# Gelu's tanh form: three ScalarE and three VectorE operations replaced by one activation and one product

## The chip, the cores and the metric

The kernel runs on one core of one Trainium2 chip. That core has five engines that matter here: TensorE (PE, with weight loads listed as PEld), VectorE (DVE), ScalarE (ACT), GpSimd (POOL) and SyncE (SP), which issues the transfers. The metric is device time of one execution in microseconds; the kernel before takes 2557.23 us, the median of three runs (2554.48 to 2558.53). Profiles come from one execution each.

## The reference

`x` is 2048 rows of 576 numbers. It is normalised (`xn`), and two branches read `xn`: an attention with 32 heads of 18 numbers, and a gated feed-forward with 4608 hidden numbers. The result joins them:

```python
def _gelu(x):
    return jax.nn.gelu(x, approximate=True)
def _B_ref(x, w_gate, w_up, w_down):
    return (_gelu(x @ w_gate) * (x @ w_up)) @ w_down
xn = _layernorm(x, axis=-1)
s = _A_ref(xn, A_wqkv, A_wo)
g = _silu(_B_ref(xn, B_w_gate, B_w_up, B_w_down))
return x + s * g
```

With `approximate=True`, gelu(g) is 0.5 g (1 + tanh(0.79788 (g + 0.044715 g^3))). The silu is y sigmoid(y), which equals 0.5 y (1 + tanh(y / 2)).

## The kernel before

**Stages.** A prologue normalises and transposes `x` and projects q, k and v (to DRAM). Then come 144 feed-forward *sections*: 4 blocks of 512 rows, times 18 parts of 256 hidden numbers, times 2 halves (`g` 0 and 1) of 128. The first 11 sections run alone or with a few attention maxima; the next 128 each carry a quarter of one of 32 attention units (4 heads by 512 queries); the last 5 are in the epilogue, with the output projection.

**One section with attention.** PE runs 27 pairs of matmuls into `pgu`, one PSUM tile of two banks: `pg` (gate sums) and `pu` (up sums). Among them `spread` places 8 score pairs (`pe`, line 897) and 8 pairs for row maxima (`pm`, line 851). ACT takes each `pe` with an Exp of 128x1024 into `pT` (line 898); DVE takes each `pm` with a maximum reduction (line 852). At the end PE multiplies the 16 probability tiles with the values into `acc` (line 914). In the first quarter of a unit `acc` is put away by a ScalarE Copy (line 918), in the other three it is added to `accs` on DVE (line 920).

**Down projection.** After every second section, the halves of a part being complete, PE runs seven products `py` (line 525), which DVE adds to the seven sums `M` (line 575); in the first part of a block ScalarE or DVE copies them (lines 573, 571). `sums_a` and `cut_a` form the operands of these products from `h` on POOL (lines 456 to 461 and 447, 448). While the first block (and some parts of the second) runs, the section that also holds the down products forms its down weights: three ScalarE Copies into `T` (lines 495, 497, 498), the last of which has to wait until the products have read the old `T`. The 32 maxima of a unit are closed by lines 858, 861, 862 and a DVE transpose (867), one hand to the other, on DVE, POOL and DVE.

**PSUM.** `pgu`, `pe`, `pm`, `acc` and `py` share one ring of four tiles (`ring`, `RING = 4`). `pgu` holds a tile through its section and until `activate` has read it for the last time.

**The place of the change.** `activate` turns `pgu` into `h` at the end of each section: Square of `pg` (ACT, line 428); (square + 1/GC) times `pg` (DVE, 429); a Copy of `pu` out of PSUM (ACT, 432), times `pg` (DVE, 433), which frees the ring tile; Tanh with scale GC GS (ACT, 434); (tanh + 1) times that product (DVE, 436). The result is twice gelu(gate) times up. So `M` holds twice the sums of the reference, and silu's Tanh has scale 0.25, its product the factor 0.25. `last_section` in the epilogue does the same with three DVE operations behind the Square and the Tanh (lines 1130 to 1134).

**What sets the order.** PE's and SP's orders are those of the program text. ACT, DVE and POOL are ordered by a planner from its own costs in attention (`keep_in_program_order` fixes some places), by the program text in the epilogue.

Of the kernel before, what the change touches and what calls it, by code (L numbers as in the profile page):

```python
# [8 lines left out]
F32 = mybir.dt.float32  # L9
F32R = mybir.dt.float32r  # L10
AF = mybir.ActivationFunctionType
ALU = mybir.AluOpType
# [5 lines left out]
P = 128  # L18
NT = S // P
TB = 512  # L20
# [36 lines left out]
ADD, SUB = ALU.add, ALU.subtract  # L57
COMBINED = (((6, ADD, 0), (5, ADD, 0)), ((6, SUB, 3), (5, ADD, 2)), ((6, SUB, 4), (5, SUB, 1)), ((4, ADD, 2), (1, SUB, 3)))
EPS = 1e-5
GC = 0.044715  # L60
GS = 0.7978845608028654
SCALE = DH ** -0.5


# [24 lines left out]
def kernel(ctx: ExitStack, tc: tile.TileContext, x, wqkv, wo, w_gate, w_up, w_down, out):  # L89
# [331 lines left out]

        return [lambda i=i: pair(i) for i in range(len(terms))], pg, pu

    def activate(pg, pu, g, early):

        h = ffn.tile([P, 3 + 3 * g, TH], F32, name=f"h{g}", bufs=2 - g)
        t1 = h[:, 0:2].rearrange("p a t -> p (a t)")
        nc.scalar.activation(t1, pg, AF.Square)
        nc.vector.scalar_tensor_tensor(t1, t1, 1.0 / GC, pg, op0=ALU.add, op1=ALU.mult)  # L429
        if early:  # L430
            t2 = ffn.tile([P, TB], F32, name="t2", bufs=1)
            nc.scalar.activation(t2, pu, AF.Copy)  # L432
            nc.vector.tensor_tensor(t2, t2, pg, op=ALU.mult)  # L433
        nc.scalar.activation(t1, t1, AF.Tanh, scale=GC * GS)
        if early:
            FF["last"] = lambda: nc.vector.scalar_tensor_tensor(t1, t1, 1.0, t2, op0=ALU.add, op1=ALU.mult)
        else:
            nc.vector.scalar_tensor_tensor(t1, t1, 1.0, pg, op0=ALU.add, op1=ALU.mult)
            nc.vector.tensor_tensor(t1, t1, pu, op=ALU.mult)
        return h  # L440


# [173 lines left out]
    def section(specials=(), slots=False):  # L616

        n = FF["n"]
        FF["n"] += 1
        b, r = divmod(n // G, NR)  # L620
        g = n % G
        keep = tc.keep_in_program_order
        pairs, pg, pu = gate_up()
        hooks, FF["hooks"] = FF["hooks"], {}

        def hook(i, what):
            hooks.setdefault(i, []).append(what)

        for i in range(n + 1, min(n + 3, NF)):
            if i not in FF["raw"]:  # L630
                FF["raw"][i] = load_gu(gu_part(i))
        nxt = FF["raw"].pop(n + 1, None)
        one = split_ap if n + 1 < ATT.start else split
        if nxt:
            for k in range(NG - 1):
                split_gu(nxt, k, one)
        if n == 0:
            load_rawd(0)
        if g == 0 and (b, r) in FORMED:
            raw = FF["rawd"]  # L640
            hook(12, lambda: sums_b(raw))
        new = n + 1 < NF and (n + 1) % (NR * G) == 0
        xd = []
        if new:
            for k in range(NG - 1):
                hook(9 * k + 9, lambda k=k: xd.append(load_xd(b + 1, k)))
        for p in spread(pairs, specials, 1 if slots else None, hooks):
            p()
        if nxt:
            split_gu(nxt, NG - 1, one)  # L650
        if n == 0:
            cut_plain_b(FF["rawd"])
        FF["w"] = nxt
        FF["act"] = activate(pg, pu, g, n < ATT.stop)
        if g > 0 or n not in ATT:
            FF.pop("last", lambda: None)()
        if new:
            xd.append(load_xd(b + 1, NG - 1))
            for t in hooks.get(len(pairs), ()):
                t()  # L660
            FF["xd"] = xd
# [5 lines left out]
    def finish():  # L667

        n = FF["n"] - 1
        b, r = divmod(n // G, NR)  # L670
        g, h, s = n % G, FF["act"], part(b, r)
        pool, vec, act = nc.gpsimd, nc.vector, nc.scalar
        keep = tc.keep_in_program_order
        FF.pop("last", lambda: None)()

        def hook(i, what):
            FF["hooks"].setdefault(i, []).append(what)

        def behind(what):
            what(keep if (n + 1) % (NR * G) == 0 else lambda i: i)  # L680

        late = (n + 2) % (NR * G) == 0 and n + 2 < NF
        if g == 1 and (b, r + 1) in NEXT:
            load_rawd(part(b, r + 1))
        if b == 0 and r < PLAIN:
            if g == 0 and r > 0:
                raw = FF["rawd"]
                hook(4, lambda: cut_plain_b(raw))
            cut_plain(g, h)
        elif (b, r) in FORMED:  # L690
            lead = n < ATT.start
            if g == 0:
                if lead:
                    hook(6, lambda: high_b(0))
                    hook(12, lambda: high_b(1))
                else:
                    high_b(0)
                    high_b(1)
                hook(9 if lead else 2, lambda: low_b(0))
                hook(16 if lead else 10, lambda: low_b(1))  # L700
                for k, i in enumerate((19, 24) if lead else (1, 3) if late else (13, 20)):
                    hook(i, lambda k=k: t_piece(s, k, True))
                sums_a(g, h, vec if lead else pool)
                hook(12, lambda: cut_a(0, h, pool, pool, keep))
            else:
                for k, i in enumerate((2, 9)):
                    hook(i, lambda k=k: t_piece(s, 2 + k, True))
                behind(lambda k: (sums_a(g, h, pool, k), cut_a(1, h, pool, pool, keep)))
        else:
            if g == 0:  # L710
                for k, i in enumerate((None, 5, 27, 27) if late else (None, 5, 13, 21)):
                    if i is None:
                        t_piece(s, k)
                    else:
                        hook(i, lambda k=k: t_piece(s, k))
            behind(lambda k: (sums_a(g, h, pool, k), cut_a(g, h, pool, pool, k)))
        if g == G - 1:
            FF["down"].append((b, r, n + 1))
# [54 lines left out]
    def gate(k, i):  # L773

        y, t = (t[:, i] for t in SC)
        nc.scalar.activation(t, y, AF.Tanh, scale=0.25)
        nc.gpsimd.tensor_tensor(t, t, y, op=ALU.mult)
        nc.gpsimd.tensor_tensor(y, y, t, op=ADD)

# [227 lines left out]
    with tc.tile_pool(name="epi", bufs=1, reuse_waits="tile") as epi:  # L1007
# [45 lines left out]
        def gate(k):  # L1053
            if gated <= k < len(groups) and groups[k][0] < NB - 1:
                yy = YY[k % len(YY)]
                th = ffn.tile([P, D], F32, name="th", tag="h0", bufs=2)
                act.activation(th, yy, AF.Tanh, scale=0.25)
                vec.scalar_tensor_tensor(yy, th, 1.0, yy, op0=ADD, op1=ALU.mult)

        def project(k):  # L1060
# [11 lines left out]
        def multiply(k, po, c):  # L1072
            b, j = groups[k]
            t = YY[k % len(YY)].rearrange("p (c d) -> p c d", c=2)
            if b < NB - 1:
                vec.scalar_tensor_tensor(t[:, c], t[:, c], 0.25, po[:, c, 0:DC], op0=ALU.mult, op1=ALU.mult)
            else:
                for i in range(2)[c]:
                    m = QUARTERS[2 * (j // 2) + i][2]
                    vec.scalar_tensor_tensor(t[:, i], FF["M"][:, m, j % 2], 0.25, po[:, i, 0:DC], op0=ALU.mult, op1=ALU.mult)  # L1080

        def finish_rows(k, c):
            t, xx = (a[k % len(a)][:, DC * c.start:DC * c.stop] for a in (YY, XX))
# [26 lines left out]
        def last_section():  # L1110

            n = FF["n"]
            FF["n"] += 1
            g = n % G
            pairs, pg, pu = gate_up()
            hooks, FF["hooks"] = FF["hooks"], {}
            nxt = FF["raw"].pop(n + 1, None)
            if nxt:
                split_gu(nxt, 0)
                split_gu(nxt, 1)  # L1120
            for t in spread(pairs, (), 1, hooks):
                t()
            if nxt:
                split_gu(nxt, 2)
            FF["w"] = nxt
            h = ffn.tile([P, 3 + 3 * g, TH], F32, name=f"h{g}", bufs=2 - g)
            t1 = h[:, 0:2].rearrange("p a t -> p (a t)")

            def gelu():
                act.activation(t1, pg, AF.Square)  # L1130
                vec.scalar_tensor_tensor(t1, t1, 1.0 / GC, pg, op0=ADD, op1=ALU.mult)
                act.activation(t1, t1, AF.Tanh, scale=GC * GS)
                vec.scalar_tensor_tensor(t1, t1, 1.0, pg, op0=ADD, op1=ALU.mult)
                vec.tensor_tensor(t1, t1, pu, op=ALU.mult)

            return h, gelu
# [83 lines left out]
        gate(n)  # L1220
        for i, c, m in QUARTERS:
            t = ffn.tile([P, 2, DC], F32, name="tg", tag=("h0", "h1")[c], bufs=2 - c)
            act.activation(t, M[:, m], AF.Tanh, scale=0.25)
            vec.scalar_tensor_tensor(M[:, m], t, 1.0, M[:, m], op0=ADD, op1=ALU.mult)
            for k in range({6: 1, 4: 2}.get(m, 0)):
                step()
# [30 lines left out]
```

## Time and profile before

| | |
|---|---|
| median of three runs | 2557.23 us |
| the profiled execution | 2556.38 us, its span 2554.6 us |
| granted TensorE clock | 0.998 |
| PE busy / PEld busy | 2533.5 us (99%) / 1873.7 us (73%) |
| DVE busy | 2079.9 us (81%) |
| ACT busy | 1453.3 us (57%) |
| POOL busy | 1622.6 us (64%) |

Busy time is summed over the span. A group's row in the profile gives its line, engine and operation, the tiles it writes and reads, how often it ran, its busy time, the mean of one in ns, and the engine's idle time just before it with what ended that idleness. A row of the timeline gives start, duration, engine, line, operation and count; in brackets stands the engine's idle time before it.

### The profile page before, as it was taken

What the parts mean: (1) busy time and instruction counts of PE and PEld (TensorE: products, weight loads), DVE (VectorE), ACT (ScalarE), POOL (GpSimd) and SP (SyncE); (2) the same over time, 40 slices, a digit from 0 to 9 for tenths busy, and PEclk for the clock granted to TensorE, in tenths of its full rate; (3) what the DMA queues carried; (4) which work ended last, traced back from release to release, by engine and by line L of the source; (5) the groups of instructions that cost most, each with busy time, mean ns of one, the idle gap of its engine ahead of it and who ended that gap; (6) DMA issues with size and microseconds to landing.
All of it is one profiled execution on the core that took longest, in us unless ns stands there. A gap on an engine that the chain in (4) does not pass through costs nothing.

```text
span 2554.6 us, 58761 instructions
## 1 busy us (share of the span) xinstructions
PE 2533.5 (99%) x23434; PEld 1873.7 (73%) x23434; DVE 2079.9 (81%) x2371; ACT 1453.3 (57%) x1753; POOL 1622.6 (64%) x1684
## 2 busy tenths in 40 slices
PE   9999999999999999999999999999999999999999
PEld 8888877777677777777676776777676777777689
DVE  5327888888898888888887888888888888889357
ACT  3224466666666665655556555666555656566631
POOL 3005688888888865566657555666657666666773
PEclk9999999999999999999999999999999999999999
DMA  8965455655585556676676776766667676665676
GB/s 258 313 205 141 113 171 171 167 158 163 165 248 163 164 166 157 160 166 163 166 223 168 172 174 159 174 169 170 154 159 227 164 173 164 169 168 155 188 192 231
DMA packets 416648, 455.39 MB, mean 178 GB/s; under 512 B 109428, under 2 KB 289396, under 8 KB 416376
## 3 DMA queue, kind: packets, MB, share of 16 engines
q1 hardware_dynamic: 416376, 451.64, 65.5%
q8 instruction: 186, 3.05, 0.5%
q14 instruction: 86, 0.70, 0.1%
HBM read 354.38 MB, written 97.13 MB: 177 GB/s over the span
## 4 chain that ended last, share of the span: by engine, by line
PE 88%; DMA 5%; POOL 4%; DVE 2%; issue 1%; SPq 1%; ACT 0%; POOLq 0%; DVEq 0%
PE pgu L419 31%; PE acc L914 16%; PE py L525 15%; PE pm L851 8%; PE pe L897 8%; PE po L193 6%; DMA raw<-in_B_w_up_dram 4%; PE po L1068 2%; POOL wl L119 1%; PE py L588 1%; POOL M L602 1%; POOL wh L117 1%; POOL h L459 1%; DVE mx L852 1%; DMA KA<-qk 1%
## 5 line engine op out<-in xcount | busy, mean ns | idle before, releaser
L898 ACT ACTIVATE pT<-pe 128x1024 f32<-128x1024 f32 x1024 | 1048.2, 1027 | 520.9 <-PE pe L897 491.6
L852 DVE TENSOR_REDUCE mx<-pm 128x2 f32<-128x1024 f32 x1024 | 1218.6, 1224 | 111.6 <-PE pm L851 102.4
L419 PE MATMUL pgu<-xd,wh 64*128 64x512 f32 x5184 | 975.6, 393 | 0.0
L419 PEld LDWEIGHTS pgu<-xd,wh 64*128 64x128 f32 x5184 | 527.9, 185 | 108.9 <-issue 39.9
L419 PE MATMUL pgu<-xd,wl 64*128 64x512 f32 x2592 | 529.3, 390 | 0.2 <-POOL wl L124 0.2
L117 POOL TENSOR_SCALAR wh<-raw 128x384 fp32r<-128x384 f32 x402 | 217.4, 541 | 454.1 <-DMA raw<-in_B_w_up_dram 239.9
L914 PE MATMUL acc<-pT,VS 128*32 128x512 f32 x4096 | 466.0, 595 | 0.0
L897 PE MATMUL pe<-QT,KA 64*128 64x512 f32 x2048 | 427.0, 396 | 12.8 <-DVE mx L852 12.0
L119 POOL TENSOR_TENSOR wl<-raw,wh 128x384 fp32r<-128x384 f32 x402 | 417.0, 1038 | 32.9
L851 PE MATMUL pm<-KA,QT 64*128 64x512 f32 x2048 | 428.3, 397 | 0.9 <-PE pgu L419 0.6
L525 PE MATMUL py<-T,ah 64*128 64x288 f32 x3848 | 389.8, 294 | 0.0
L575 DVE TENSOR_TENSOR M<-py,M 128x576 f32<-128x576 f32 x448 | 332.9, 756 | 41.9 <-PE py L525 29.8
L525 PEld LDWEIGHTS py<-T,ah 64*128 64x128 f32 x3848 | 313.7, 184 | 53.6 <-issue 52.8
L448 POOL TENSOR_TENSOR al<-h,ah 128x512 fp32r<-128x512 f32 (+1 forms) x143 | 295.4, 2065 | 51.0 <-ACT ah L445 40.1
L914 PEld LDWEIGHTS acc<-pT,VS 128*32 128x32 f32 x4096 | 120.1, 109 | 276.7 <-issue 229.7
L525 PE MATMUL py<-T,al 64*128 64x288 f32 x1924 | 290.8, 291 | 0.0
L419 PEld LDWEIGHTS pgu<-xd,wl 64*128 64x128 f32 x2592 | 262.7, 185 | 35.9 <-POOL wl L124 0.7
L897 PEld LDWEIGHTS pe<-QT,KA 64*128 64x128 f32 x2048 | 193.2, 184 | 127.6 <-DVE mx L852 31.6
L851 PEld LDWEIGHTS pm<-KA,QT 64*128 64x128 f32 x2048 | 212.4, 185 | 44.5 <-DVE M L575 11.4
L525 PEld LDWEIGHTS py<-T,al 64*128 64x128 f32 x1924 | 188.3, 185 | 0.0
L433 DVE TENSOR_TENSOR t<-t,pgu 128x512 f32<-128x512 f32 x139 | 95.6, 688 | 92.3 <-ACT t L432 92.3
L432 ACT ACTIVATE t<-pgu 128x512 f32<-128x512 f32 x139 | 83.0, 597 | 137.7 <-DVE h L429 137.7
(151 smaller groups left out, 2248.3 us busy)
## 6 DMA issues: line engine op xcount, KB each, us to landing
T<-ts SPq DMA_DIRECT2D x98, 576.0 KB
KA<-qk SPq DMA_DIRECT2D x768, 72.0 KB
T<-ts SPq DMA_DIRECT2D x98, 432.0 KB
raw<-in_B_w_gate_dram SPq DMA_DIRECT2D x144, 288.0 KB
raw<-in_B_w_up_dram SPq DMA_DIRECT2D x144, 256.0 KB
ts<-T SPq DMA_DIRECT2D x36, 576.0 KB
VS<-vs SPq DMA_DIRECT2D x128, 152.0 KB
qk<-t SPq DMA_DIRECT2D x72, 256.0 KB
```

The source lines that it names most:

```text
L117: first = nc.gpsimd.tensor_scalar(hi, raw, 1.0, 1.0, op0=ALU.mult, op1=ALU.mult)
L119: keep(nc.gpsimd.tensor_tensor(lo, raw, f(hi), op=ALU.subtract))
L193: nc.tensor.matmul(o, st, m, start=(i == 0), stop=(i == len(terms) - 1))
L419: nc.tensor.matmul(o, w[1 + wp][k][rr, c, :], xd[k][xp][rr, c, :], start=(i == 0), stop=(i == len(terms) - 1))
L448: low = two.tensor_tensor(lo, raw, f(hi), op=ALU.subtract)
L525: one = nc.tensor.matmul(py[:, t, 0:DC], h[rr, a, t * P:(t + 1) * P], T[rr, w, k], start=x == 0 and n == 0, stop=x == 1 and n == len(terms ...
L575: nc.vector.tensor_tensor(M[:, m], py[:, :, 0:DC], M[:, m], op=ALU.add)
L851: nc.tensor.matmul(pm[:, a], QS[u, r][rr, t * P:(t + 1) * P], KS[(u * NA + c) % KB][r][rr, :], start=True, stop=True)
L852: nc.vector.tensor_reduce(MX[u][:, 2 * r:2 * r + 2, t, c], pm, axis=AX.X, op=ALU.max)
L897: nc.tensor.matmul(pe[:, a], KS[(u * NA + c) % KB][r][rr, t * P:(t + 1) * P], QS[u, r][rr, :], start=True, stop=True)
L898: nc.scalar.activation(PT[u, kt][:, 2 * r:2 * r + 2, :], pe, AF.Exp, scale=SCALE)
L914: nc.tensor.matmul(ACC[u][32 * a:32 * a + 32, :], VS[(u * NA + c) % VB][:, v:v + 32], pt[:, a, :], start=first, stop=last, skip_group_chec ...
```

## The change

`activate` becomes one ScalarE activation, `Gelu_apprx_tanh` of `pg` into `h`, and one DVE product of `h` with `pu` from PSUM, emitted in the section itself; the Copy of `pu` and its tile `t2`, the Square, the Tanh and two DVE operations go, and so does the closure `FF["last"]`, by which the last product was emitted later. `last_section` gets the same two operations. Since `h` is now the product without the factor 2, the four Tanh operations of silu take scale 0.5 in place of 0.25, and the factor 0.25 in `multiply` becomes 0.5.

```diff
-    def activate(pg, pu, g, early):
+    def activate(pg, pu, g):
 
         h = ffn.tile([P, 3 + 3 * g, TH], F32, name=f"h{g}", bufs=2 - g)
         t1 = h[:, 0:2].rearrange("p a t -> p (a t)")
-        nc.scalar.activation(t1, pg, AF.Square)
-        nc.vector.scalar_tensor_tensor(t1, t1, 1.0 / GC, pg, op0=ALU.add, op1=ALU.mult)
-        if early:
-            t2 = ffn.tile([P, TB], F32, name="t2", bufs=1)
-            nc.scalar.activation(t2, pu, AF.Copy)
-            nc.vector.tensor_tensor(t2, t2, pg, op=ALU.mult)
-        nc.scalar.activation(t1, t1, AF.Tanh, scale=GC * GS)
-        if early:
-            FF["last"] = lambda: nc.vector.scalar_tensor_tensor(t1, t1, 1.0, t2, op0=ALU.add, op1=ALU.mult)
-        else:
-            nc.vector.scalar_tensor_tensor(t1, t1, 1.0, pg, op0=ALU.add, op1=ALU.mult)
-            nc.vector.tensor_tensor(t1, t1, pu, op=ALU.mult)
+        nc.scalar.activation(t1, pg, AF.Gelu_apprx_tanh)
+        nc.vector.tensor_tensor(t1, t1, pu, op=ALU.mult)
         return h
...
-        FF["act"] = activate(pg, pu, g, n < ATT.stop)
-        if g > 0 or n not in ATT:
-            FF.pop("last", lambda: None)()
+        FF["act"] = activate(pg, pu, g)
...
-        FF.pop("last", lambda: None)()
...
-        nc.scalar.activation(t, y, AF.Tanh, scale=0.25)
+        nc.scalar.activation(t, y, AF.Tanh, scale=0.5)
...
             def gelu():
-                act.activation(t1, pg, AF.Square)
-                vec.scalar_tensor_tensor(t1, t1, 1.0 / GC, pg, op0=ADD, op1=ALU.mult)
-                act.activation(t1, t1, AF.Tanh, scale=GC * GS)
-                vec.scalar_tensor_tensor(t1, t1, 1.0, pg, op0=ADD, op1=ALU.mult)
+                act.activation(t1, pg, AF.Gelu_apprx_tanh)
                 vec.tensor_tensor(t1, t1, pu, op=ALU.mult)
```

More of the change, by code (lines that the diff above doesn't have):

```diff
@@ L59 @@
 EPS = 1e-5
-GC = 0.044715
-GS = 0.7978845608028654
 SCALE = DH ** -0.5
@@ L1056, in gate @@
                 th = ffn.tile([P, D], F32, name="th", tag="h0", bufs=2)
-                act.activation(th, yy, AF.Tanh, scale=0.25)
+                act.activation(th, yy, AF.Tanh, scale=0.5)
                 vec.scalar_tensor_tensor(yy, th, 1.0, yy, op0=ADD, op1=ALU.mult)
@@ L1075, in multiply @@
             if b < NB - 1:
-                vec.scalar_tensor_tensor(t[:, c], t[:, c], 0.25, po[:, c, 0:DC], op0=ALU.mult, op1=ALU.mult)
+                vec.scalar_tensor_tensor(t[:, c], t[:, c], 0.5, po[:, c, 0:DC], op0=ALU.mult, op1=ALU.mult)
             else:
@@ L1079, in multiply @@
                     m = QUARTERS[2 * (j // 2) + i][2]
-                    vec.scalar_tensor_tensor(t[:, i], FF["M"][:, m, j % 2], 0.25, po[:, i, 0:DC], op0=ALU.mult, op1=ALU.mult)
+                    vec.scalar_tensor_tensor(t[:, i], FF["M"][:, m, j % 2], 0.5, po[:, i, 0:DC], op0=ALU.mult, op1=ALU.mult)
         def finish_rows(k, c):
@@ L1222 @@
             t = ffn.tile([P, 2, DC], F32, name="tg", tag=("h0", "h1")[c], bufs=2 - c)
-            act.activation(t, M[:, m], AF.Tanh, scale=0.25)
+            act.activation(t, M[:, m], AF.Tanh, scale=0.5)
             vec.scalar_tensor_tensor(M[:, m], t, 1.0, M[:, m], op0=ADD, op1=ALU.mult)
```

## The prediction

> **What bounds the kernel now.** I read the page first.
>
> ```profile
> span 2554.6 us, 58761 instructions
> PE 2533.5 (99%) x23434; PEld 1873.7 (73%) x23434; DVE 2079.9 (81%) x2371; ACT 1453.3 (57%) x1753; POOL 1622.6 (64%) x1684
> PE 88%; DMA 5%; POOL 4%; DVE 2%; issue 1%; SPq 1%; ACT 0%; POOLq 0%; DVEq 0%
> ```
>
> PE is busy all but 21 us of the span, and the chain that ended last runs on PE for 88% and through ACT for 0%. So taking work off ACT and DVE buys little by itself, but whatever makes PE wait is paid in full. The question is what the change does to the moments at which PE waits for ACT or DVE. So next come the groups of the two engines, shapes kept apart.
>
> ```profile
> L898 ACT ACTIVATE pT<-pe 128x1024 f32<-128x1024 f32 x1024 | 1048.2, 1027 | 520.9 <-PE pe L897 491.6
> L434 ACT ACTIVATE h<-h 128x512 f32<-128x512 f32 x139 | 86.6, 623 | 0.0
> L432 ACT ACTIVATE t<-pgu 128x512 f32<-128x512 f32 x139 | 83.0, 597 | 137.7 <-DVE h L429 137.7
> L428 ACT ACTIVATE h<-pgu 128x512 f32<-128x512 f32 x139 | 82.6, 594 | 30.0 <-PE pgu L419 29.6 <-issue 0.5
> L918 ACT ACTIVATE accs<-acc 128x512 f32<-128x512 f32 x32 | 19.2, 599 | 27.5 <-PE acc L914 27.5
> L498 ACT ACTIVATE T<-rawd 128x576 fp32r<-128x576 f32 x18 | 12.4, 688 | 7.3 <-PE py L525 7.3
> L573 ACT ACTIVATE M<-py 128x576 f32<-128x576 f32 x14 | 8.9, 651 | 5.9 <-PE py L525 4.6
> L228 ACT ACT_TABLE_LOAD x1 | 1.3, 1283 | 0.7 <-PEq L1243 0.7
> L356 ACT ACT_TABLE_LOAD x1 | 1.3, 1283 | 0.0
> ...
> L436 DVE SCALAR_TENSOR_TENSOR h<-h,t 128x512 f32<-128x512 f32 x139 | 112.2, 807 | 14.8 <-DVE t L433 0.5
> L433 DVE TENSOR_TENSOR t<-t,pgu 128x512 f32<-128x512 f32 x139 | 95.6, 688 | 92.3 <-ACT t L432 92.3
> L429 DVE SCALAR_TENSOR_TENSOR h<-h,pgu 128x512 f32<-128x512 f32 x139 | 94.2, 678 | 48.5 <-ACT h L428 48.5
> ```
>
> Two things are to be seen. The three ACT and three DVE operations of line 428 to 436 run 139 times. And there are two table loads in the whole run, 1283 ns each, although Exp, Tanh, Square and Copy take turns 128 times: these four come out of one loaded table. Then I read ACT's timeline at the two loads.
>
> ```profile
> 0.72 1.28 ACT L228 ACT_TABLE_LOAD   x1 [0.72 <-PEq L1243]
> 8.02 0.30 ACT L228 ACTIVATE st<-st,eps 128x4 f32<-128x4 f32 x1 [6.01 <-DVE st L226]
> ...
> 152.98 0.41 ACT L324 ACTIVATE vn<-po 128x288 f32<-128x288 f32 x1 [1.46 <-PE po L193]
> 153.41 1.28 ACT L356 ACT_TABLE_LOAD   x1
> 154.70 0.20 ACT L356 ACTIVATE eps<-eps 128x1 f32<-128x1 f32 x1
> ```
>
> The first load ran at 0.72 while its Sqrt waited until 8.02: a load doesn't share the wait of the activation that it serves. The second was needed when the first Tanh came after Sqrt; Copy and Identity had run under Sqrt's table for 150 us. It began 0.02 us behind the Copy before it (152.98 + 0.41 = 153.39), and Tanh began 0.01 us behind it: a switch costs 1.31 us from end to start.
>
> **The change part by part.** *Removed.* ACT loses lines 432 and 434 (83.0 + 86.6 us), DVE lines 429 and 436 (94.2 + 112.2); the epilogue's five repeats are some 10 us more on both engines together. Line 428 becomes Gelu, with its shape, so I price it at its 0.59 us; line 433 becomes the product, 0.69. None of this is on PE's chain. The scales of 0.5 for 0.25 cost nothing, being the same instructions.
>
> *Added: switches.* No row shows Gelu. Either it lies in the table that serves Exp, then there is no load, or it doesn't, then every attention section, having eight Exps, one Gelu and the next eight Exps, has two. The nearest rows are those of Tanh and Exp (no load between them) and of Sqrt and Tanh (one load). I take two loads, since a table that served only the simple functions beside its own curve was the reason for the one switch seen, and Gelu is another curve; 128 sections make 256, plus one in the first sections: 257 x 1.283 = 330 us more on ACT. ACT would come to 1453 - 173 + 330 = 1610 us, still 63% of the span, so the total decides nothing; the places do. The Trainium skill, page ScalarE: Activation LUTs, section Table sets, lists exp and tanh in one set, as the loads here agree, and says that gelu's set is separate from that of gelu_apprx_tanh; no run so far shows it.
>
> *Where a section's end has room.* A section without down products and without a Copy at its end:
>
> ```profile
> 1214.79 2.13 ACT L898 ACTIVATE pT<-pe 128x1024 f32<-128x1024 f32 x2 [0.41 <-PE pe L897]
> 1216.88 0.60 ACT L428 ACTIVATE h<-pgu 128x512 f32<-128x512 f32 x1
> 1218.93 0.62 ACT L434 ACTIVATE h<-h 128x512 f32<-128x512 f32 x1
> 1221.11 2.12 ACT L898 ACTIVATE pT<-pe 128x1024 f32<-128x1024 f32 x2 [1.56 <-PE pe L897]
> ...
> 1207.29 1.03 ACT L898 ACTIVATE pT<-pe 128x1024 f32<-128x1024 f32 x1 [7.09 <-PE pe L897]
> ...
> 1219.07 0.69 DVE L433 TENSOR_TENSOR t<-t,pgu 128x512 f32<-128x512 f32 x1 [0.66 <-ACT t L432]
> 1219.86 0.70 DVE L436 SCALAR_TENSOR_TENSOR h<-h,t 128x512 f32<-128x512 f32 x1
> ```
>
> The last Exp ends at 1216.92. The new order: load to 1218.22, Gelu to 1218.82, Exp's load at once, to 1220.12. The next Exp starts at 1221.11, when PE has its scores: both loads are covered, with 1.0 us left. The cover is PE's products with the values; without it the second load would cost up to 1.31. After a section with down products ACT idles 7.09 us, cover enough. The product runs on DVE from 1218.84 to 1219.53: `pgu`'s ring tile comes free 0.2 us earlier than now (1219.76), and `h` 1.0 us earlier (1220.56).
>
> *Where there is no room.* A load stands right before the activation that needs it (line 356), and Copy needs none. So a Copy between Gelu and the first Exp keeps Exp's load behind it. There are three kinds, one row of Copy and Exp each for the first two:
>
> ```profile
> 456.03 0.60 ACT L918 ACTIVATE accs<-acc 128x512 f32<-128x512 f32 x1 [0.86 <-PE acc L914]
> 456.72 2.12 ACT L898 ACTIVATE pT<-pe 128x1024 f32<-128x1024 f32 x2
> 457.15 4.89 DVE L852 TENSOR_REDUCE mx<-pm 128x2 f32<-128x1024 f32 x4 [0.97 <-PE pm L851]
> 458.07 0.40 PE L851 MATMUL pm<-KA,QT 64*128 64x512 f32 x2
> ...
> 442.36 0.69 ACT L498 ACTIVATE T<-rawd 128x576 fp32r<-128x576 f32 x1 [0.42 <-PE py L525]
> 442.96 2.15 ACT L898 ACTIVATE pT<-pe 128x1024 f32<-128x1024 f32 x2
> 443.38 1.23 DVE L852 TENSOR_REDUCE mx<-pm 128x2 f32<-128x1024 f32 x1
> 444.27 0.47 PE L851 MATMUL pm<-KA,QT 64*128 64x512 f32 x2
> ```
>
> (a) Line 918 puts `acc` away in 32 sections. The Copy ends at 456.63, the load at 457.94 instead of Exp's start at 456.72: the first Exp is 1.22 us late. (b) Line 498 runs 18 times, 17 of them in attention, and waits for the last down product, so no cover is left: 443.05 + 1.31 = 444.36 instead of 442.96, 1.40 late. (c) Line 573's 14 Copies are the end of two down projections, priced as (b).
>
> What is queued behind the late Exp is all other Exps, and PE waits for them through the ring: `pgu`, the first `pe`, the first `pm` and the second `pe` hold the four tiles, so the second `pm` needs the first one freed. In (a) the first Exp ends at 456.72 + 1.03 = 457.75 and that matmul starts at 458.07, a slack of 0.32; in (b) 443.99 and 444.27, 0.28. So PE stalls 0.90 and 1.12 us a time. Once it has, the Exps (1.03) run faster than PE asks for them (8 in some 10 us), so nothing adds up, and PE, being the bound, doesn't win it back.
>
> Bounds for one stall: no slack at all, 1.22 and 1.40, together 32 x 1.22 + 19 x 1.40 = 66 us. On the other side, the second `pm` could be given the tile of the first `pm`, which its reduction frees at 457.15 + 1.22 = 458.37 and 443.38 + 1.23 = 444.61; then it stalls 0.30 and 0.34, together 16 us. I take the middle mechanism, 32 x 0.90 + 19 x 1.12 = 50 us, since a tile freed first in the old order is the one a planner assigns. Line 776's Tanh of the gate, ten times, lies in pauses of the 7.09 kind and gets 0, at most 10 x 1.4 = 14.
>
> *What comes earlier.* `h` 1.0 us earlier lets POOL begin its sums earlier, and POOL delays the closing of the maxima:
>
> ```profile
> DVE mt L867 <- POOL m L862: 15.3, 12, 3.6
> ```
>
> At most 12 x 1.0 = 12 us, at least nothing, since some of these waits come from late weights; I take 6. The moved product (emitted in the section, no longer deferred) changes no queue I can name: line 436 already ran right behind line 433.
>
> *Sum:* 2556.4 (the profiled execution's own time) + 50 - 6 = 2600 us; the median of the runs is 0.9 us above that execution, so 2600 stands for it too. Own range: 2556 + 16 - 6 = 2566 to 2556 + 66 = 2622.
>
> The Trainium skill, page ScalarE: Activation LUTs, section What ACT_TABLE_LOAD costs, adds a drain of about 1380 ns to each load, 2.66 us a switch; the rows at 153 us contradict it with 1.31, and by it the time would be near that of the third rival.
>
> **The rivals.** *No late Exp* (the other side): Gelu shares Exp's table, or Exp's load is put right behind Gelu, ahead of the Copies. Then every load is covered by the 1.0 us shown, no Exp is late, and only the earlier `h` counts: 2556 - 6 = 2550, between 2544 and 2556. It decides as soon as Exp's load ends before the Copy. For it: the chain holds ACT at 0%, and Exp and Tanh do share a table. Against: Sqrt and Tanh don't, and the one load seen stands right before its user.
>
> *The load waits with its Exp*, for the scores. Then 32 plain sections and 45 with down products lose 1.31 - 0.3 = 1.0 each as well: 2600 + 77 = 2677. Against it is the load at 0.72.
>
> *A switch costs twice its row*, 2.57 us. Then in a plain section Exp's table is there at 1222.7, 1.6 late, stall 1.3, 32 times; (a) stalls 2.2, (b) and (c) 2.4: 41 + 70 + 46 = 157, less 6, makes 2707. Against it is Tanh's start at 154.70.
>
> **How the numbers follow.** Forecast 0.66; no late Exp 0.17; load waiting 0.07; double switch 0.07; the planner, with changed costs, reordering something unforeseen 0.03. The predicted time is 2600. For 8 in 10 the range goes from 2543, which takes in nearly all of the first rival, to 2640, beyond the upper bound of 2622 for the gate's Tanh. No change means within 0.2%, 5 us, which is about what a measurement of this kernel can tell. Faster has 0.10 and same 0.08 (the first rival, divided, and little of the rest), slower 0.82.
>
> **What would show it.** About 259 table loads; ACT near 1610 us, DVE near 2080 - 94 - 112 - 7 = 1867; behind every Copy of line 918 a load and an Exp 1.31 us after the Copy's end; PE's idle time up from 21 to some 65 us, by waits for line 898; plain sections as long as now. Two loads alone would mean the first rival. The sum is wrong if such loads stand and PE doesn't wait, or if sections without Copies grow too.

## The result, and the profile after

The changed kernel takes 2637.97 us (median, 2636.81 to 2639.95) against 2555.86 us for the kernel before, timed beside it: a ratio of 1.0322, 95% interval 1.0304 to 1.0340. It is slower by 82 us; 44 had been forecast (2600). Its page, of a span of 2635.2 us:

```profile
span 2635.2 us, 58569 instructions
PE 2601.5 (99%) x23434; PEld 1817.3 (69%) x23434; DVE 1898.3 (72%) x2083; ACT 1609.6 (61%) x1727; POOL 1600.6 (61%) x1684
PE 86%; DVE 10%; issue 1%; ACT 1%; POOL 1%; DMA 1%; SPq 0%; POOLq 0%; DVEq 0%; ACTq 0%
```

ACT gained 156 us of work, as worked out; DVE lost 182 of the 213 that had been worked out (1867 us forecast), and where the other 31 went was not followed up. PE, with the same 23434 matmuls and a granted clock of 1.000 (0.998 before), is shown busy 68 us longer, so part of its stalls seems to be counted as busy here, and its idle time (34 us, before 21, forecast 65) to understate them. DVE's share of the chain rose from 2% to 10%. The groups of the new operations, shapes apart (busy us, mean ns, then ACT's idle time before and who ended it):

```profile
L426 ACT ACT_TABLE_LOAD x129 | 165.5, 1283 | 2.3
L883 ACT ACT_TABLE_LOAD x128 | 164.2, 1283 | 369.0 <-PE pe L882 365.8 <-PE pgu L417 0.4
L426 ACT ACTIVATE h<-pgu 128x512 f32<-128x512 f32 x139 | 83.1, 598 | 41.7 <-PE pgu L417 40.3
```

There are 257 more loads, as forecast (Gelu is line 426 now, Exp 883), and Gelu costs 598 ns, about what the Square did (594). The new thing is the second row: ACT stood idle 365.8 us *in front of Exp's loads*, waiting for PE's scores. A plain section, the front of one after down products, and one behind the Copy of `acc` (line 903 now), on ACT's timeline:

```profile
1326.08 2.14 ACT L883 ACTIVATE pT<-pe 128x1024 f32<-128x1024 f32 x2 [0.42 <-PE pe L882]
1328.24 1.28 ACT L426 ACT_TABLE_LOAD   x1
1329.53 0.60 ACT L426 ACTIVATE h<-pgu 128x512 f32<-128x512 f32 x1
1332.37 1.28 ACT L883 ACT_TABLE_LOAD   x1 [2.24 <-PE pe L882]
1333.66 2.86 ACT L883 ACTIVATE pT<-pe 128x1024 f32<-128x1024 f32 x3
...
1352.49 1.28 ACT L883 ACT_TABLE_LOAD   x1 [7.79 <-PE pe L882]
1353.78 2.86 ACT L883 ACTIVATE pT<-pe 128x1024 f32<-128x1024 f32 x3
...
1366.39 0.60 ACT L903 ACTIVATE accs<-acc 128x512 f32<-128x512 f32 x1 [1.59 <-PE acc L899]
1367.07 1.28 ACT L883 ACT_TABLE_LOAD   x1
1368.36 2.86 ACT L883 ACTIVATE pT<-pe 128x1024 f32<-128x1024 f32 x3
```

The load ahead of Gelu begins as the last Exp ends. The load ahead of Exp doesn't begin behind Gelu at 1330.13, where the prediction put it; it sits out 2.24 us, or 7.79 us after down products, until the scores are there, and only then takes its 1.28. So the first Exp is 1.3 us late also in the sections without a Copy, which the prediction had at no cost: 76 of these 77 loads waited for scores, the 365.8 us of the row above. The one exception is the load ahead of the very first Exp:

```profile
299.59 0.60 ACT L426 ACTIVATE h<-pgu 128x512 f32<-128x512 f32 x1 [5.09 <-PE pgu L417]
300.20 1.28 ACT L883 ACT_TABLE_LOAD   x1
306.41 1.02 ACT L883 ACTIVATE pT<-pe 128x1024 f32<-128x1024 f32 x1 [4.93 <-PE pe L882]
```

That load ran ahead, as the prediction assumed for all. The trace says why the others don't. It also holds wait instructions (EVENT_SEMAPHORE, of ACT's queue, ACTq). These are the instructions of line 883 from 1331 to 1334 us, each with its count, its duration in ns (least, median, most) and its start:

```profile
L883 ACTq EVENT_SEMAPHORE  x1: 17/17/17, 1332.3 to 1332.3; - x1
L883 ACT ACT_TABLE_LOAD  x1: 1283/1283/1283, 1332.4 to 1332.4; - x1
L883 ACT ACTIVATE pT<-pe x1: 1024/1024/1024, 1333.7 to 1333.7; 128x1024 f32<-128x1024 f32 x1
```

In the packed trace the wait instruction names PE's semaphore, the load none, the Exp that of ACT itself. An Exp that waits for two things, PE's scores and an earlier ACT instruction, carries one of the two waits; the other stands ahead of the load. It is so at 127 of the 128 loads of line 883. The very first Exp waits for PE alone, carries that wait, and its load has nothing ahead of it. Gelu is no exception: in 83 of its 129 places one or two wait instructions stand ahead of its load, but they had been met by then (2.3 us of idle time in all).

The stall shows on PE in the section behind line 903 at 530 us:

```profile
531.67 0.39 PE L882 MATMUL pe<-QT,KA 64*128 64x512 f32 x2
532.29 2.86 ACT L883 ACTIVATE pT<-pe 128x1024 f32<-128x1024 f32 x3
532.72 0.18 PEld L836 LDWEIGHTS pm<-KA,QT 64*128 64x128 f32 x2 [0.63 <-DVE mx L837]
533.37 0.19 PEld L882 LDWEIGHTS pe<-QT,KA 64*128 64x128 f32 x2 [0.35 <-ACT pT L883]
534.28 0.19 PEld L836 LDWEIGHTS pm<-KA,QT 64*128 64x128 f32 x2 [0.38 <-ACT pT L883]
```

The second `pm` waits for the reduction that frees the first `pm`'s ring tile, then `pe` and `pm` wait for the late Exps: three short waits. They come in plain sections too; over the whole run (us, times, longest):

```profile
PEld pm L836 <- DVE mx L837: 75.2, 123, 0.6
PEld pe L882 <- ACT pT L883: 43.2, 124, 0.7
```

In the kernel before the first of these came once, with 0.3 us, and the second not at all. These are waits of weight loads, which overlap matmuls, so their sum is not PE's loss.

### The profile page after: what moved, and what is told of

The parts are those of the page before. It is cut to its first block, busy times and chain, and to the rows that moved or that the text cites. A ratio compares the mean times of both kernels' runs of the same rounds, so it can differ in the third digit from the quotient of the medians.

```text
span 2635.2 us, 58569 instructions
## 1 busy us (share of the span) xinstructions
PE 2601.5 (99%) x23434; PEld 1817.3 (69%) x23434; DVE 1898.3 (72%) x2083; ACT 1609.6 (61%) x1727; POOL 1600.6 (61%) x1684
## 4 chain that ended last, share of the span: by engine, by line
PE 86%; DVE 10%; issue 1%; ACT 1%; POOL 1%; DMA 1%; SPq 0%; POOLq 0%; DVEq 0%; ACTq 0%
PE pgu L417 29%; PE acc L899 17%; PE py L513 12%; PE pm L836 10%; PE pe L882 8%; PE po L191 7%; DVE mx L837 5%; DVE M L563 4%; PE po L1053 2%; PE py L576 1%; ACT L883 1%; ACT pT L883 0%; DMA raw<-in_B_w_up_dram 0%; PE pt L261 0%; POOL M L590 0%
## 5 line engine op out<-in xcount | busy, mean ns | idle before, releaser
L883 ACT ACTIVATE pT<-pe 128x1024 f32<-128x1024 f32 x1024 | 1019.7, 1027 | 150.8 <-PE pe L882 128.9
L417 PE MATMUL pgu<-xd,wh 64*128 64x512 f32 x5184 | 951.4, 392 | 0.0
L417 PEld LDWEIGHTS pgu<-xd,wh 64*128 64x128 f32 x5184 | 502.7, 185 | 116.0 <-issue 36.5
L115 POOL TENSOR_SCALAR wh<-raw 128x384 fp32r<-128x384 f32 x402 | 207.0, 515 | 530.4 <-PE pgu L417 293.8
L417 PE MATMUL pgu<-xd,wl 64*128 64x512 f32 x2592 | 517.0, 390 | 0.0
L836 PE MATMUL pm<-KA,QT 64*128 64x512 f32 x2048 | 438.3, 421 | 22.2 <-DVE mx L837 21.2
L117 POOL TENSOR_TENSOR wl<-raw,wh 128x384 fp32r<-128x384 f32 x402 | 407.4, 1014 | 32.8
L883 ACT ACT_TABLE_LOAD x128 | 164.2, 1283 | 369.0 <-PE pe L882 365.8
L836 PEld LDWEIGHTS pm<-KA,QT 64*128 64x128 f32 x2048 | 197.1, 184 | 166.2 <-DVE mx L837 75.2
L417 PEld LDWEIGHTS pgu<-xd,wl 64*128 64x128 f32 x2592 | 250.4, 185 | 44.4
L427 DVE TENSOR_TENSOR h<-h,pgu 128x512 f32<-128x512 f32 x139 | 95.6, 688 | 197.1 <-ACT h L426 197.1
```

What stands on the lines that cost most here:

```text
L115: first = nc.gpsimd.tensor_scalar(hi, raw, 1.0, 1.0, op0=ALU.mult, op1=ALU.mult)
L117: keep(nc.gpsimd.tensor_tensor(lo, raw, f(hi), op=ALU.subtract))
L417: nc.tensor.matmul(o, w[1 + wp][k][rr, c, :], xd[k][xp][rr, c, :], start=(i == 0), stop=(i == len(terms) - 1))
L836: nc.tensor.matmul(pm[:, a], QS[u, r][rr, t * P:(t + 1) * P], KS[(u * NA + c) % KB][r][rr, :], start=True, stop=True)
L883: nc.scalar.activation(PT[u, kt][:, 2 * r:2 * r + 2, :], pe, AF.Exp, scale=SCALE)
```

## The experiments

Two theories were set against each other. W: the load waits with the Exp it serves, and the late first Exp stalls PE. G: the loads as such cost the time, by ACT's 330 us or by the load ahead of Gelu, which delays `h` and the release of `pgu`. The first four ran together, beside the kernel before (2556.81 us there), the last two in a second session (2555.13).

**An early Exp behind Gelu.** A small Exp that waits for no scores draws the load to itself:

```diff
         FF["act"] = activate(pg, pu, g)
+        if n + 1 in ATT:
+            col = ffn.tile([P, TB], F32, name="t2", bufs=1)
+            behind(nc.scalar.activation(col[:, 0:1], ident[:, 0:1], AF.Exp), FF["gelu"])
```

(`FF["gelu"]` is the Gelu instruction; `behind` orders the small Exp after it.)

> The changed kernel plus one Exp of 128x1, ahead of every attention section, that waits for no scores and is ordered right behind Gelu, so that the load of Exp's table no longer carries the wait for the scores. Theory W (the load waits with the Exp it serves, and the late first Exp stalls PE): first Exps start as in the kernel before, the 0.7 to 1.0 us a section go, and the earlier h is left as a gain of some 17 us: 2535 to 2550 us. Rival G (the load ahead of Gelu, or 330 us more of loads on ScalarE, costs the time): above 2600 us, since all loads are still there.

Measured: 2550.31 us, ratio to the kernel before 0.9972 (0.9960 to 0.9984). ACT's groups and timeline in this kernel:

```profile
L426 ACT ACT_TABLE_LOAD x129 | 165.5, 1283 | 2.5 <-issue 0.2
L645 ACT ACT_TABLE_LOAD x128 | 164.2, 1283 | 2.3
...
1279.88 1.28 ACT L426 ACT_TABLE_LOAD   x1
1281.17 0.60 ACT L426 ACTIVATE h<-pgu 128x512 f32<-128x512 f32 x1
1281.79 1.28 ACT L645 ACT_TABLE_LOAD   x1
1283.08 0.20 ACT L645 ACTIVATE t<-ident 128x1 f32<-128x1 f32 x1
1284.06 2.12 ACT L886 ACTIVATE pT<-pe 128x1024 f32<-128x1024 f32 x2 [0.77 <-PE pe L885]
```

All 257 loads are still there, now with 2.3 instead of 369 us of idle time ahead of Exp's, and the first Exp waits 0.77 us for PE: ACT is ready before the scores. With the same loads and the same arithmetic 88 us are gone, so G falls. W holds as far as that the late first Exp is what costs the time; whether each load was late by its wait is taken up with the last two kernels. It is also the fastest of these kernels with the whole computation, by 0.3% over the kernel before.

**No loads: Tanh in place of Gelu.**

```diff
-        nc.scalar.activation(t1, pg, AF.Gelu_apprx_tanh)
+        nc.scalar.activation(t1, pg, AF.Tanh)
...
```

(The same in `last_section`.)

> The changed kernel with Tanh in place of Gelu (so the gate's function is not computed): the same two instructions and no load in attention. Both theories: 2535 to 2550 us, the gain of the fewer operations and the earlier h alone. W: within 5 us of the run with the early Exp. G: 50 us or more below it.

Measured: 2550.62 us, ratio 0.9974 (0.9964 to 0.9985). Its page shows what is left of ACT's work:

```profile
PE 2528.4 (99%) x23434; PEld 1870.4 (74%) x23434; DVE 1877.9 (74%) x2083; ACT 1294.4 (51%) x1470; POOL 1600.0 (63%) x1684
```

ACT has 367 us less to do than with the early Exp (1661.4 us there), and the time is the same to 0.3 us, where the intervals of both ratios leave some 3 us each way. A covered load costs nothing that can be seen here. And this is all that the removal of operations is worth: 6 us. Both runs lie just above the upper end of what was expected, 2550 us, by 0.3 and 0.6 us, because the gain of 17 us behind that range was too high.

**The loads with the old operations.** The kernel before with Gelu in place of the Square:

```diff
-        nc.scalar.activation(t1, pg, AF.Square)
+        nc.scalar.activation(t1, pg, AF.Gelu_apprx_tanh)
```

> The kernel before with Gelu in place of the Square (so the gate's function is not computed): its six operations stay, the two loads a section come. W: every first Exp 1.3 us late, PE stalled 0.7 to 1.0 us in 123 sections, no gain from an earlier h: 2640 to 2680 us. G: the load ahead of the Square delays the release of the gate's sums by 1.3 us too: more than 2680 us.

Measured: 2671.37 us, ratio 1.0447 (1.0429 to 1.0464), inside W's range and 9 us below where G's begins. Its loads, a wait, and one section's end on ACT's timeline:

```profile
L898 ACT ACT_TABLE_LOAD x128 | 164.2, 1283 | 247.9 <-PE pe L897 247.0
...
POOL h L459 <- DVE h L436: 167.3, 60, 4.8
...
1276.05 0.60 ACT L428 ACTIVATE h<-pgu 128x512 f32<-128x512 f32 x1
1277.40 0.60 ACT L432 ACTIVATE t<-pgu 128x512 f32<-128x512 f32 x1 [0.76 <-DVE h L429]
1277.90 0.62 ACT L434 ACTIVATE h<-h 128x512 f32<-128x512 f32 x1
1278.93 1.28 ACT L898 ACT_TABLE_LOAD   x1 [0.41 <-PE pe L897]
```

The loads alone, put where the compiler puts them, cost 115 us. The changed kernel has the same loads and is 33 us faster, more than the 6 that the removed operations are worth without loads: where the chain to `h` is long *and* begins with a load, POOL waits longer for `h`, 167.3 us here. In the kernel before that row was:

```profile
POOL h L459 <- DVE h L436: 80.9, 42, 2.2
```

That the 33 us (27 beyond those 6) come by this row is argued, not shown.

**The placing that the prediction assumed.** The small Exp, behind the last Copy where there is one, else behind Gelu, so that the load doesn't wait for scores:

```diff
             finish()
+            if n + 1 < NU * NA:
+                col = ffn.tile([P, TB], F32, name="t2", bufs=1)
+                behind(nc.scalar.activation(col[:, 0:1], ident[:, 0:1], AF.Exp), FF["gelu"])
```

(`FF["gelu"]` is set anew by each of the three Copies.)

> The changed kernel with the small Exp ordered behind the last Copy before the first Exp (lines 918, 498, 573 of the kernel before), right behind Gelu where there is none: the placing that the prediction assumed, a load behind the Copies that does not wait for the scores. W: 32 x 0.9 + 19 x 1.0 = 48 us above the run with the early Exp, 2583 to 2598 us. If the slack of the ring was misjudged instead of the wait, it is as slow as the changed kernel, 2638 us.

Measured: 2606.86 us, ratio 1.0193 (1.0178 to 1.0208); 56.5 us above the run with the early Exp, not 48, and 9 above the expected range. A section behind the Copy of `acc`:

```profile
461.25 0.60 ACT L904 ACTIVATE accs<-acc 128x512 f32<-128x512 f32 x1 [1.57 <-PE acc L900]
461.87 1.28 ACT L990 ACT_TABLE_LOAD   x1
463.17 0.20 ACT L990 ACTIVATE t<-ident 128x1 f32<-128x1 f32 x1
463.27 1.92 ACT L884 ACTIVATE pT<-pe 128x1024 f32<-128x1024 f32 x2
464.33 0.19 PEld L837 LDWEIGHTS pm<-KA,QT 64*128 64x128 f32 x2 [1.28 <-ACT pT L884]
464.33 0.50 PE L837 MATMUL pm<-KA,QT 64*128 64x512 f32 x2 [0.85 <-ACT pT L884]
```

So the world that the prediction described does give about its 2600. The second `pm` waits for the first Exp, by 0.85 us for its matmul (0.90 had been worked out) and 1.28 us for its weights. Some 0.1 us a section is the small Exp's own: it starts at 463.17, the first Exp at 463.27. In the changed kernel the same `pm` waited for the first reduction instead, 0.63 us: another ring tile.

**The two halves of the sections.** The early Exp, but only ahead of sections that begin without a Copy, and in a second kernel only ahead of those that begin behind one (`and copies`). The first, against the kernel with the early Exp everywhere:

```diff
+        copies = n in ATT and ((n - ATT.start) % NA == 0 or g == 0 and (b, r) in FORMED or n % (NR * G) == G and b > 1)
-        if n + 1 in ATT:
+        if n + 1 in ATT and not copies:
```

> The changed kernel with the small early Exp only ahead of the 77 sections at whose front no Copy stands; the 51 behind Copies keep a load that waits for the scores. If each section pays for its own late Exp and nothing is won back elsewhere, the 51 sections cost 32 x 0.9 + 19 x 1.0 = 48 us over the run with all Exps early (2550): 2590 to 2605 us. If the sections without Copies cost nothing in the changed kernel, as the prediction had it: 2638 us.

Measured: 2590.03 us, ratio 1.0135 (1.0120 to 1.0150). ACT's loads in this kernel:

```profile
L646 ACT ACT_TABLE_LOAD x77 | 98.8, 1283 | 1.4
L887 ACT ACT_TABLE_LOAD x51 | 65.4, 1283 | 3.2 <-PE pgu L417 0.4
```

> The complement: the small early Exp only ahead of the 51 sections that begin behind a Copy; the 77 others keep a load that waits. If the wait is the cause there, they cost what the changed kernel has beyond the 48 us of the others, 88 - 48 = 40 us over 2550: 2580 to 2600 us, and the two runs' excesses add up to 88. By the prediction these loads are covered: 2550 us.

Measured: 2595.33 us, ratio 1.0150 (1.0133 to 1.0167), the kernel before at 2555.13 beside both:

```profile
L887 ACT ACT_TABLE_LOAD x77 | 98.8, 1283 | 367.7 <-PE pe L886 351.5 <-PE pgu L417 16.1
L646 ACT ACT_TABLE_LOAD x51 | 65.4, 1283 | 0.9
```

The split is clean: 51 loads left behind Copies cost 2590.0 - 2550.3 = 40 us, 0.78 a section; the 77 left without a Copy ahead cost 2595.3 - 2550.3 = 45 us, 0.58 a section. Together 85, of the 88 that lie between the changed kernel and the one with the early Exp. With each kernel taken against the kernel before of its own session, it is 41 and 47, together 88 of 89. The stalls split in the same way: the second `pm` waits for the reduction 50 times in the first kernel and 73 in the second, of the 123 in the changed one:

```profile
PEld pm L840 <- DVE mx L841: 30.8, 50, 0.6
...
PEld pm L840 <- DVE mx L841: 44.3, 73, 0.6
```

Two causes make an Exp late. The 51 loads behind Copies stood idle 3.2 us in all, the 77 others 367.7. Behind a Copy it is the Copy that holds the load back, as the prediction had it, and when the Copy is done the scores are there; with a load that doesn't wait for scores in that place the time was no shorter (2606.86 us). In the other sections it is the wait instruction ahead of the load. So the wait of theory W accounts for the 77 sections, and the Copies for the 51.

## Why the prediction was right and wrong

The direction, the count of loads (259 with the first two), their 1283 ns, Gelu's price, ACT's total and the place of the damage (a late first Exp stalls PE through the ring) came out. The sum came to half of the loss, 44 us of 82: one step fell, which left out a term of 45 us, and one term, the 50 us behind Copies, was 10 too high. Put together from the runs it is 2556 + 40 + 45 - 6 = 2635 us.

That 2638 us lies within the stated 2543 to 2640 is luck. The working's own bounds end at 2622; the rest was room for the gate's Tanh, which no run sets apart, and not for the sections that did pay. The prediction named the sign of being wrong that came: sections without Copies grew too.

*"A load doesn't share the wait of the activation that it serves"* failed. It rested on one row, the load at 0.72 ahead of a Sqrt that started at 8.02. That Sqrt waits for one thing (DVE) and carries that wait itself, behind its load; the first Exp of a section waits for two, and one of the two waits stands ahead of the load. The prediction had this as a rival, "the load waits with its Exp", at 0.07, and turned it down by that same row. The split stood in the trace of the kernel before already: there too 127 of the 128 first Exps had a wait instruction for PE ahead of them and carried the wait for ACT. The missing term is 45 us for the 77 sections. The rival's own price, 77 us, was too high: it took 1.0 us a section where 0.58 was measured.

*Plain sections have 1.0 us left.* True as arithmetic: with the early Exp 0.77 us are left behind both loads and the small Exp's 0.20. But the load didn't start when ACT was free.

*The stall behind Copies, 50 us,* was measured at 40 with the load as the changed kernel has it, at 56 in the placing that the prediction described, both between its bounds of 16 and 66. The term hangs on which ring tile the second `pm` gets; the prediction took the first `pe`'s. The waits show the first `pm`'s tile in the changed kernel and the first `pe`'s with the small Exp. By that tile the changed kernel would be at the lower bound of 16; but "nothing adds up" failed there, since in the section at 530 us two more waits follow the first, of 0.35 and 0.38 us. How much of each reaches PE isn't shown, and why the planner chose differently wasn't tried.

*The gain of 6 us* has the right size, 6.5 us in the run with the early Exp, but not by the row named for it: DVE's wait for POOL ahead of the transpose went from 15.3 to 13.7 us there.

```profile
DVE mt L855 <- POOL m L850: 13.7, 8, 4.8
```

Where the rest comes from is open.

*The rivals.* "No late Exp" was priced at 2550, and that is what the kernel is worth once its loads start in time, by either way named: no load, or Exp's load ahead of the Copies. "A switch costs twice its row" is out: in the changed kernel the next activation starts 0.01 us behind the load at 257 of the 259 loads, the other two being those whose user waited. The Trainium skill, page ScalarE: Activation LUTs, section What ACT_TABLE_LOAD costs, puts a drain of about 1380 ns on top of the load. These 257 loads show none, and the load at 153.41 us of the kernel before took 1.31 us from the Copy's end at 153.39 to the next start.

## What to carry to other kernels

Before replacing several operations by one activation function, look whether it lives in the same table as the function that it alternates with; if not, count two loads a turn, and ask of each not what it costs but *when it may start*. One of the waits of the activation behind it can stand ahead of a load that the compiler inserts, and then idle time in front of it is no cover; a tiny activation of the needed function without that wait, placed where the engine falls idle, restores the cover for 0.2 us. One row in which a load ran ahead says how that one was waited for, not how the next will be: compare the number of waits of the two activations, and look for wait instructions ahead of the one that will get the load.

## What the runs showed of the hardware that had not been expected

A table load can be free: 257 of them, 330 us of ACT's time, changed the time by less than a measurement can tell (2550.31 against 2550.62 us without any in attention). Where an activation with two waits needs a load, one wait stands ahead of the load (127 of 128 loads of Exp), and the load is held with it. No load came for Tanh and Copy beside Gelu: in the kernel before with Gelu as its Square, Copy and Tanh run between Gelu at 1276.05 us and Exp's load at 1278.93, and the loads stayed at two a section.
